# Listing a branch's loads, fixing its buffers in one tile, adding free slots, moving a product earlier and joining copies in a two-branch forward and backward kernel

## Chip, cores, metric

One core of one Trainium2 chip. The metric is the device time of one execution in microseconds (us). "1907.7 (3 runs)" is a median.

## What is computed

The reference runs a forward pass and its gradients (bf16, S = 2048, D = 1024, F = 3584), cut here to what matters:

```python
def _A_ref(q, k, v, shift_k, ssm_k, ssm_D):      # branch A: long convolution by FFT
    k_shift = ...                                # four taps over time
    kv = k_shift * v
    y_f = rfft(pad(kv)) * rfft(pad(ssm_k))       # per channel, length 2*S
    y = irfft(y_f)[:S] + kv * ssm_D
    return q * y
def _B_ref(x, W_gate, W_up, W_down):             # branch B: gated MLP
    gate, up = x @ W_gate, x @ W_up
    return (relu(gate) * up) @ W_down
xn = _layernorm(x)
out = x + _A_ref(xn, ...) + _B_ref(xn, ...)      # then the gradients of all inputs but B_x
```

## The kernel before

Both branches run on one core. The dense branch B fills TensorE with rows of eight matmuls of 512 columns: `hidden` has, for 14 blocks of weights, eight rows each of gate, up and a gradient row, and reloads the weights over a block's last rows; `grad_down` and `grad_in` follow, then the output phase (ps_o) and the input gradient (ps_x). Branch A computes its transforms as small matmuls ("passes"), for eight groups of 128 channels. It is a generator of slots, and each slot gives at most one pass for TensorE and one piece for VectorE. The dense branch counts the matmul time that it has issued, and a slot of A is taken every 1900 ns of it (`SLOT`), later every 1760 or 1250 (`DENSE`, with or without a pass). The instructions of both keep the order in which they are issued.

```python
    def run(f): ...                       # calls f, or takes the next piece of a generator
    SLOT, DENSE = 1900, (1760, 1250)
    def steps(self):
        ...
        for gi in range(self.NG):
            st = nx
            for p, d in self.slots(st, gi):          # p: pass on TensorE, d: piece on VectorE
                self.run(p)
                self.run(d)
                yield self.DENSE[p is None] if self.dense else self.SLOT
            nx = st.get("nx")
```

The loads of the next group are issued in the group's slots, wherever these fall in a block of the dense branch. Both branches issue on one queue, from SyncE:

```python
    def slots(self, st, gi):
        ...
        nx = None if last else self.load_filter(gi + 1)        # four loads of hn
        f2 = self.fwd2_pair()
        yield f2, None
        yield None, none if last else lambda: self.load_g(nx)
        yield f2, None
        yield None, none if last else lambda: self.load_xn(nx)
        # ... cut ...
        yield None, flg                                        # flip: two transposes on VectorE
        yield None, flg
        yield None, q                                          # q: a piece of a complex product
        yield ibg, q                                           # second inverse pass, reads the flips
        # ... cut ...
        yield lambda: self.tap_sums(st), q                     # sums into a PSUM tile
        if not last:
            flH = self.flip_H(nx)
            yield None, self.both(lambda: self.add_D(nx), flH)
            self.load_k(nx)
            yield None, flH
        yield None, lambda: self.tap_diagonals(st)             # reads that tile: "dg"
        Cy, Ch = self.inv_tile(), self.inv_tile()
        ia = self.inv_a_pair((Ch, Cy))                         # four passes, two PSUM tiles each
        ...
        yield ia, tg
        # ... cut: the product K*H, whose last piece stands in the slot before ...
        yield ia, tk
        # ... cut ...
        yield None, flK
        yield None, flK                                        # the next group's first pass follows
```

A's PSUM pool `ps` has two tiles. Its transform buffers B, C and GKV come from a pool of three rotating buffers, `big`; spectra and flipped data lie in a tile `arena`. The evacuation of a paired inverse pass:

```python
    self.big = self.pool("a_big", 3, side=R)
    ...
            for h in range(2):
                for k in range(2):
                    self.act(Cs[k][:, :, 2 * h:2 * h + 2, 2 * j:2 * j + 2, :],
                             ps[h][:, :, :, k].rearrange("p q m b (cp i) -> p (b cp) q m i", i=2))
```

The lines of the profile point to helpers: L72 is every matmul of A, L76 its ScalarE copies, L80 its VectorE operations, L306 its transposes, L88 its loads, L905 the rows of `hidden`.

## Time and profile before

| | before |
|---|---|
| median of 3 runs | 1907.69 us (1907.53 to 1908.38) |
| the profiled execution | 1910.69 us, span 1908.9 us |
| TensorE busy | 1884.1 us of the span |
| VectorE, ScalarE busy | 1051.5 us, 619.3 us |
| mean granted clock | 0.997 |

TensorE is the bound. So the lines to read are its waits, the time after a wait, and, where a DMA ended a wait, what stood ahead of that DMA in the queue. The prediction below shows them. "Idle before" in a group or timeline counts from the modelled end of a matmul. To size a loss I also compared starts: the time from one matmul's start to the next, less the normal step of that pair of kinds (216 ns between two 512-column matmuls, 309 from one of those to most passes, or the median of that kind of pass). I call this the start-to-start loss. The granted clock is the share of TensorE's full clock in the profile's clock record; "half clock" is a stretch recorded at 0.50.

### The profile page before, as it was taken

The page shows a single profiled execution, that of the slowest core. Times are in us where ns is not written, and L with a number is a line of the kernel's source. Part 1 is how long each engine was busy: PE and PEld are TensorE (multiplying, and loading weights), DVE is VectorE, ACT ScalarE, POOL GpSimd, SP SyncE. Part 2 cuts the span into 40 slices and gives each one's busy share as a digit, 9 for nine tenths or more (in the row PEclk, how much of TensorE's full clock was granted, in tenths as well). Part 3 has the DMA queues.
Part 4 walks back from the last instruction along what each step waited for, and adds up shares of the span by engine and source line. Part 5 has one row for each costly group of instructions (what it writes and reads, how often), then busy time and mean ns, then how long its engine had stood idle before and what let it go on. Part 6 is the DMA issues. An engine that isn't in the chain of part 4 may idle for free.

```text
span 1908.9 us, 32808 instructions
## 1 busy us (share of the span) xinstructions
PE 1884.1 (99%) x13720; PEld 855.2 (45%) x13720; DVE 1051.5 (55%) x1544; ACT 619.3 (32%) x922; POOL 14.9 (1%) x37
## 2 busy tenths in 40 slices
PE   9999999999999999999999999999999999999999
PEld 4444444344444444444444444444444544444444
DVE  6676887788788795875848757100212222222222
ACT  5655345335435535455454543211000000000000
POOL 1000000000000000000000000000000000000000
PEclk9999999999999999999999999999999999999999
DMA  9897658775675874639555434772999965555543
GB/s 250 248 238 173 169 148 179 193 193 145 168 176 153 224 221 117 168 92 255 138 147 144 137 100 145 191 253 73 259 245 237 241 148 122 122 122 122 122 121 72
DMA packets 694037, 322.93 MB, mean 169 GB/s; under 512 B 524408, under 2 KB 663424, under 8 KB 693888
## 3 DMA queue, kind: packets, MB, share of 16 engines
q1 hardware_dynamic: 683392, 299.99, 63.3%
q10 hardware_dynamic: 9216, 16.65, 2.9%
q0 software_dynamic: 1280, 4.20, 0.6%
q8 instruction: 107, 1.75, 0.4%
q14 instruction: 42, 0.34, 0.1%
HBM read 143.79 MB, written 95.44 MB: 125 GB/s over the span
## 4 chain that ended last, share of the span: by engine, by line
PE 91%; DVE 5%; issue 1%; ACT 1%; DMA 1%; SPq 0%; DVEq 0%
PE ps_x L1422 20%; PE ps_w L1195 19%; PE ps_o L1353 10%; PE ps_g L905 9%; PE ps_u L905 9%; PE ps_h L905 8%; PE ps_d L1195 8%; PE ps L72 5%; PE ps_d L1208 1%; DVE arena L306 1%; DVE ru L1009 1%; ACT C L76 1%; PE ps_w L1208 0%; ACT B L76 0%; DVE ht L1011 0%
## 5 line engine op out<-in xcount | busy, mean ns | idle before, releaser
L1195 PE MATMUL ps_w<-ugs,xn_nat 128*128 128x512 bf16 x1728 | 382.4, 379 | 0.0
L905 PEld LDWEIGHTS <-xnT 128*128 128x128 bf16 x1792 | 171.4, 98 | 217.7 <-issue 16.3
L1195 PEld LDWEIGHTS <-xn_nat 128*128 128x128 bf16 x1728 | 164.9, 98 | 201.6 <-issue 8.8
L905 PE MATMUL ps_u<-wu,xnT 128*128 128x512 bf16 x896 | 209.0, 383 | 4.2 <-DMA wu<-in_B_W_up_dram 4.1
L905 PE MATMUL ps_h<-wdT,goT 128*128 128x512 bf16 x896 | 207.6, 381 | 0.0
L905 PE MATMUL ps_g<-wg,xnT 128*128 128x512 bf16 x896 | 204.4, 380 | 1.1 <-DMA wg<-in_B_W_gate_dram 0.4
L1440 ACT ACTIVATE w<-xn,m 128x512 f32<-128x512 bf16 x32 | 24.3, 806 | 553.0 <-issue 317.2
L1422 PE MATMUL ps_x<-wuT,guT 128*128 128x512 bf16 x896 | 198.6, 379 | 0.0
L1422 PE MATMUL ps_x<-wgT,ggT 128*128 128x512 bf16 x896 | 198.6, 379 | 0.0
L1353 PE MATMUL ps_o<-wd,hT 128*128 128x512 bf16 (+1 forms) x896 | 187.6, 372 | 0.0
L1195 PE MATMUL ps_d<-g_nat,hs 128*128 128x512 bf16 x768 | 172.5, 379 | 0.0
L1345 DVE TENSOR_TENSOR ya<-ya,xe 128x1024 bf16<-128x1024 bf16 x16 | 11.1, 693 | 242.4 <-DMA xe<-xn_d 242.4
L306 DVE STREAM_TRANSPOSE arena<-C 128x1024 f32<-128x1024 f32 x48 | 89.8, 1939 | 87.6 <-ACT C L76 78.3
L1422 PEld LDWEIGHTS <-guT 128*128 128x128 bf16 x896 | 87.7, 98 | 105.7
L1422 PEld LDWEIGHTS <-ggT 128*128 128x128 bf16 x896 | 87.7, 98 | 105.5
L1353 PEld LDWEIGHTS <-hT 128*128 128x128 bf16 x896 | 87.7, 98 | 100.0
L905 PEld LDWEIGHTS <-goT 128*128 128x128 bf16 x896 | 85.1, 98 | 104.2 <-issue 6.7
L1009 DVE SCALAR_TENSOR_TENSOR ru<-ru,ps_u 128x512 bf16<-128x512 bf16 x112 | 76.4, 682 | 92.6 <-issue 43.2
L1424 DVE CUSTOM_DVE_ANT_0 gx<-ps_x,gy 128x512 f32<-128x512 f32 x32 | 22.1, 692 | 185.3 <-PE ps_x L1422 185.3
L76 ACT CAST C<-ps 128x512 bf16<-128x512 f32 (+1 forms) x160 | 96.5, 682 | 81.1 <-PE ps L72 75.3
L1299 ACT CAST wi<-ps_w 128x512 bf16<-128x512 f32 x108 | 64.1, 593 | 178.8 <-PE ps_w L1195 172.6
L1103 ACT CAST gh<-ps_h 128x512 bf16<-128x512 f32 x112 | 65.8, 588 | 154.9 <-PE ps_h L905 147.9
(154 smaller groups left out, 1663.4 us busy)
## 6 DMA issues: line engine op xcount, KB each, us to landing
ug_d<-ru SPq DMA_DIRECT2D x112, 256.0 KB, 3.6
ugs<-ug_d SPq DMA_DIRECT2D x112, 256.0 KB, 5.0
wg<-in_B_W_gate_dram SPq DMA_DIRECT2D x56, 256.0 KB, 4.2
wu<-in_B_W_up_dram SPq DMA_DIRECT2D x56, 256.0 KB, 4.3
h_d<-ht SPq DMA_DIRECT2D x112, 128.0 KB, 2.0
hs<-h_d SPq DMA_DIRECT2D x56, 256.0 KB, 5.3
out_dram<-wi SPq DMA_DIRECT2D x56, 256.0 KB, 2.9
gt<-in_grad_out_dram SPq DMA_DIRECT2D x32, 256.0 KB, 3.2
```

Source lines behind the costliest of these rows:

```text
L72: self.pri.pin(self.nc.tensor.matmul(out, lhsT=lhsT, rhs=rhs, start=start, stop=stop))
L76: self.pri.pin(self.nc.scalar.copy(out=out, in_=in_))
L306: self.pri.pin(self.nc.vector.transpose(out=df[:, c0:c0 + 32, :], in_=sf[:, c0:c0 + 32, :]))
L905: self.pri.pin(self.nc.tensor.matmul(ps[:], lhsT=xT[:, kt * P:(kt + 1) * P], rhs=w(kt), start=(kt == 0), stop=(kt == self.DT - 1)), always ...
L1009: self.pri.pin(nc.vector.scalar_tensor_tensor(out=ru[s][:, 1, :], in0=ru[s][:, 0, :], scalar=0.0, in1=ps[:], op0=ALU.is_gt, op1=ALU.mult))
L1103: self.pri.pin(nc.scalar.copy(out=gh[:], in_=ps[:]))
L1195: self.pri.pin(self.nc.tensor.matmul(ps[:], lhsT=lhsT(st), rhs=rhs(st), start=(st == 0), stop=(st == self.ST - 1)))
L1299: self.pri.pin(nc.scalar.copy(out=wo[0][:, d, :], in_=ps[:]))
L1353: nc.tensor.matmul(ps, lhsT=hT[:, kt, :], rhs=self.wd[:, kt, oc], start=(kt == 0), stop=(kt == self.FT - 1))
L1422: nc.tensor.matmul(ps, lhsT=T[:, kt, :], rhs=W[:, kt, oc], start=(i == 0), stop=(i == n - 1))
L1424: V.tensor_tensor_reduce(out=gx[:, oc], in0=ps, in1=gy[:, oc], scale=1.0, scalar=0.0, op0=ALU.add, op1=ALU.add, accum_out=m[:, ob:ob + 1])
L1440: nc.scalar.activation(out=w[:, oc], in_=xn[:, oc], func=ACT.Identity, scale=m[:, 7:8], bias=m[:, 6:7])
```

## The change

It has four parts. (1) Loads of later groups go to a list; one is issued after a slot, and none while the dense branch is in the last rows of a block (`hold`); `need` issues what must be there. (2) The buffers of A's transforms become fixed parts of one tile, instead of rotating ones. (3) Free slots are put before passes, `tap_diagonals` is moved up, and a dense slot with a pass is 1900 for 1760. (4) A paired inverse pass is copied out by two joint instructions, not four. The core of the diff:

```diff
+    def later(self, f, st):
+        self.queue.append((f, st))
+    def need(self, f, st):
+        while (f, st) in self.queue:
+            self.issue()
+    def issue(self):
+        f, st = self.queue.pop(0)
+        f(st)
@@ steps
                 self.run(p)
                 self.run(d)
+                if self.queue and not self.hold():
+                    self.issue()
@@ open_arena
-        arena = self.pool("a_are", 1, side="right").tile([P, 5, NB1 * P], BF16, name="arena")
+        arena = self.pool("a_are", 1, side="right").tile([P, 8, NB1 * P], BF16, name="arena")
+        self.Bg, self.Bk, self.H, self.GKV = rows(7), rows(6), spectrum(4), spectrum(7)
+        self.Cg, self.Ch, self.Cy = half(5), half(5), half(6)
@@ inv_a_pair
-                for k in range(2):
-                    self.act(Cs[k][:, :, 2 * h:2 * h + 2, 2 * j:2 * j + 2, :],
-                             ps[h][:, :, :, k].rearrange("p q m b (cp i) -> p (b cp) q m i", i=2))
+                self.act(self.Cs[:, :, 2 * h:2 * h + 2, 2 * j:2 * j + 2, :],
+                         ps[h][:].rearrange("p q m k b (cp i) -> p (k b cp) q m i", i=2))
@@ slots
+        yield lambda: self.tap_sums(st), q
+        self.fetch(nx, self.load_k, self.load_taps)
+        yield None, lambda: self.tap_diagonals(st)
         if not last:
-            flH = self.flip_H(nx)
+            self.need(self.load_g, nx)
+            flH = self.flip_H()
             yield None, self.both(lambda: self.add_D(nx), flH)
-            self.load_k(nx)
             yield None, flH
-        yield None, lambda: self.tap_diagonals(st)
 ...
             tk, f2H = nx["tk"], self.fwd2(H, 1)
+            yield None, tk
             yield ia, tk
 ...
         yield None, flK
         yield None, flK
+        yield None, None
@@ LnMlp
             def last_rows(sp):
+                self.hold = True
 ...
+            self.hold = False
@@
-    SLOT, DENSE = 1900, (1760, 1250)
+    SLOT, DENSE = 1900, (1900, 1250)
```

Cut: the other fetches, the order of the slots around the two final passes (one more slot between their flips and them, the next group's kvt pass two slots later), and renamed tiles.

More of the change, by code (lines that the diff above doesn't have):

```diff
@@ L62, in __init__ @@
         self.out_gk, self.out_gv, self.out_gsk, self.out_gh, self.out_gsD = out_gk, out_gv, out_gsk, out_gh, out_gsD
-        self.pools, self.pin, self.dense = [], False, False
+        self.pools, self.pin, self.dense, self.queue = [], False, False, []
     def pool(self, name, bufs, **kw):
@@ L103, in open @@
         self.ts = self.pool("a_ts", 3, side=R)
-        self.big = self.pool("a_big", 3, side=R)
         self.tmp = self.pool("a_tmp", 2, side=R)
@@ L108, in open @@
         self.ps = self.pool("a_ps", 2, space=bass.MemoryType.PSUM)
+        self.big = self.pool("a_big", 3, side=R)
         self.lnx = self.pool("a_lnx", 5, side=R)
     def open_arena(self):
-        self.pools.pop().release()
-        arena = self.pool("a_are", 1, side="right").tile([P, 5, NB1 * P], BF16, name="arena")
+        for _ in range(2):
+            self.pools.pop().release()
+        arena = self.pool("a_are", 1, side="right").tile([P, 8, NB1 * P], BF16, name="arena")
         self.flp = arena[:, 0:2, :].rearrange("p e (k c) -> p e k c", c=P)
@@ L117, in open_arena @@
         self.G, self.K = self.GK[:, :, :, 0], self.GK[:, :, :, 1]
-        self.H = arena[:, 4, :].rearrange("p (g b i c) -> p g b i c", b=2, i=2, c=P)
+        spectrum = lambda i: arena[:, i, :].rearrange("p (g b i c) -> p g b i c", b=2, i=2, c=P)
+        rows = lambda i: arena[:, i, :].rearrange("p (b cp u r i) -> p b cp u r i", cp=32, u=2, r=16, i=2)
+        half = lambda i: arena[:, i, :].rearrange("p (bc q m i) -> p bc q m i", q=4, m=8, i=2)
+        self.Bh = arena[:, 6, :].rearrange("p (b x cp n i) -> p b x cp n i", x=2, cp=16, n=NB1, i=2)
+        self.Bg, self.Bk, self.H, self.GKV = rows(7), rows(6), spectrum(4), spectrum(7)
+        self.Cg, self.Ch, self.Cy = half(5), half(5), half(6)
+        self.Cs = arena[:, 5:7, :].rearrange("p s x -> p (s x)").rearrange("p (bc q m i) -> p bc q m i", q=4, m=8, i=2)
     def close(self):
@@ L246, in ttile, with load_filter, load_rows, load_rest @@
         return self.ts.tile([P, 19, P], BF16, name=name, tag="ts")
-    def load_filter(self, gi):
-        cg = slice(gi * P, (gi + 1) * P)
-        hn = self.ld.tile([P, 2, 32, NB1], BF16, name="hn")
-        hv = self.ssm_k[cg].rearrange("(h x c) (q n) -> x h q c n", h=2, x=2, n=NB1)
+    def later(self, f, st):
[6 more added lines that the diff above has]
+        f(st)
+    def load_filter(self, st):
+        st["hn"] = self.ld.tile([P, 2, 32, NB1], BF16, name="hn")
+        self.load_rows(st, 0)
+        self.later(self.load_rest, st)
+    def load_rows(self, st, h):
+        hv = self.ssm_k[st["cg"]].rearrange("(h x c) (q n) -> x h q c n", h=2, x=2, n=NB1)
         for x in range(2):
-            for h in range(2):
-                self.load(hn[64 * x:64 * x + 64, h], hv[x, h])
-        return dict(gi=gi, cg=cg, hn=hn)
+            self.load(st["hn"][64 * x:64 * x + 64, h], hv[x, h])
+    def load_rest(self, st):
+        self.load_rows(st, 1)
     def load_g(self, st):
@@ L309, in fwd1_filter @@
     def fwd1_filter(self, st):
-        B = st["Bh"] = self.big.tile([P, 2, 2, 16, NB1, 2], BF16, name="B", tag="big")
-        hn = st["hn"]
+        B, hn = self.Bh, st["hn"]
         for k in range(2):
@@ L327, in add_D, with fwd1 @@
             rows = slice(64 * h, 64 * h + 32)
-            b0 = st["Bh"][rows].rearrange("p b x cp n i -> p b (x cp) n i")[:, 0, :, 0, :]
+            b0 = self.Bh[rows].rearrange("p b x cp n i -> p b (x cp) n i")[:, 0, :, 0, :]
             self.tt(b0, b0, st["sD"][rows, rows.start:rows.start + 64].rearrange("p (cp i) -> p cp i", i=2), ALU.add)
-    def fwd1(self, st, key, src):
-        B = st[key] = self.big.tile([P, 2, 32, 2, 16, 2], BF16, name="B", tag="big")
+    def fwd1(self, B, src):
         for r0 in range(0, 16, 8):
@@ L400, in cmul, with inv_a @@
         yield
-    def inv_tile(self):
-        return self.big.tile([P, 64, 4, 8, 2], BF16, name="C", tag="big")
-    def inv_a(self, C, Q):
+    def inv_a(self):
+        C, Q = self.Cg, self.GKV
         for j0 in range(0, 4, 2):
@@ L421, in inv_a, with inv_a_pair @@
             yield
-    def inv_a_pair(self, Cs):
+    def inv_a_pair(self):
         for j in range(4):
@@ L522, in steps @@
         yield 25000
-        nx = self.load_filter(0)
+        self.sts = [dict(gi=gi, cg=slice(gi * P, (gi + 1) * P)) for gi in range(self.NG)]
+        st = self.sts[0]
+        self.load_filter(st)
+        self.issue()
         yield 3400
-        self.load_k(nx)
-        self.load_taps(nx)
+        self.load_k(st)
+        self.load_taps(st)
         yield 3400
-        self.load_g(nx)
+        self.load_g(st)
         yield 3400
-        self.load_v(nx)
+        self.load_v(st)
         yield 6800
-        self.load_xn(nx)
+        self.load_xn(st)
         self.pin = False
@@ L535, in steps @@
         self.open_arena()
-        self.begin(nx)
-        for gi in range(self.NG):
-            st = nx
-            for p, d in self.slots(st, gi):
+        self.begin(st)
+        for st in self.sts:
+            for p, d in self.slots(st, st["gi"]):
                 self.run(p)
                 self.run(d)
+                if self.queue and not self.hold():
+                    self.issue()
                 yield self.DENSE[p is None] if self.dense else self.SLOT
-            nx = st.get("nx")
         self.small_outputs()
@@ L552, in start_kvt, with flip_H, flip_B, ahead @@
         self.tt(kvt[:, 0:16, :], st["ksh"][:], st["vt"][:], ALU.mult)
-    def flip_H(self, st):
-        return self.flip(1, st["Bh"][:].rearrange("p b x cp n i -> p (b x cp) n i"))
-    def flip_B(self, st, key, half):
-        return self.flip(half, st[key][:].rearrange("p b cp u r i -> p (b cp) (u r) i"))
+    def flip_H(self):
+        return self.flip(1, self.Bh.rearrange("p b x cp n i -> p (b x cp) n i"))
+    def flip_B(self, B, half):
+        return self.flip(half, B.rearrange("p b cp u r i -> p (b cp) (u r) i"))
     def flip_C(self, C, half):
-        return self.flip(half, C[:].rearrange("p cp q m i -> p cp (q m) i"))
+        return self.flip(half, C.rearrange("p cp q m i -> p cp (q m) i"))
+    def ahead(self, st, k):
+        gi = st["gi"] + k
+        return self.sts[gi] if gi < self.NG else None
+    def fetch(self, st, *fs):
+        if st is not None:
+            for f in fs:
+                self.later(f, st)
     def first(self, st):
-        tk, f1h = st["tk"], self.fwd1_filter(st)
+        tk, f1h, nx = st["tk"], self.fwd1_filter(st), self.ahead(st, 1)
         yield f1h, None
@@ L567, in first @@
         yield f1h, tk
+        self.fetch(nx, self.load_filter)
         yield None, self.both(lambda: self.add_D(st), tk)
         yield None, tk
-        flH = self.flip_H(st)
+        flH = self.flip_H()
         yield None, flH
@@ L576, in first @@
         yield f2H, lambda: self.gate_grad(st)
+        self.fetch(nx, self.load_xn)
         yield None, tk
         yield f2H, lambda: self.start_kvt(st)
-        f1g, f1k = self.fwd1(st, "Bg", st["gt"]), self.fwd1(st, "Bk", st["kvt"])
+        f1g, f1k = self.fwd1(self.Bg, st["gt"]), self.fwd1(self.Bk, st["kvt"])
         yield f1g, None
@@ L582, in first @@
         yield f1g, None
+        self.fetch(nx, self.load_g)
         yield None, None
         yield f1k, None
-        flG = self.flip_B(st, "Bg", 0)
+        flG = self.flip_B(self.Bg, 0)
         yield None, flG
@@ L588, in first @@
         yield None, None
-        flK = self.flip_B(st, "Bk", 1)
+        flK = self.flip_B(self.Bk, 1)
         yield None, flK
         yield None, flK
+        yield None, None
     def slots(self, st, gi):
-        last = gi + 1 == self.NG
-        G, K, H = self.G, self.K, self.H
+        G, K, H, GKV = self.G, self.K, self.H, self.GKV
         if gi == 0:
             yield from self.first(st)
-        nx = None if last else self.load_filter(gi + 1)
-        st["nx"] = nx
-        none = lambda: None
+        nx, n2 = self.ahead(st, 1), self.ahead(st, 2)
+        last = nx is None
         f2 = self.fwd2_pair()
         yield f2, None
-        yield None, none if last else lambda: self.load_g(nx)
+        yield None, None
         yield f2, None
-        yield None, none if last else lambda: self.load_xn(nx)
+        yield None, None
         yield f2, None
         yield None, lambda: self.turn(G, 0, -1, slice(0, 4))
-        GKV = self.big.tile([P, 8, 2, 2, P], BF16, name="GKV", tag="big")
-        Cg = self.inv_tile()
         q = self.cmul(H, G, True, GKV, 0)
@@ L616, in slots @@
         yield None, lambda: self.turn(G, 0, -1, slice(4, 8))
-        iaG = self.inv_a(Cg, GKV)
+        iaG = self.inv_a()
         q = self.cmul(H, G, True, GKV, 1)
@@ L620, in slots @@
         yield None, q
-        f1h = None if last else self.fwd1_filter(nx)
+        f1h = None
+        if not last:
+            self.need(self.load_filter, nx)
+            self.need(self.load_rest, nx)
+            f1h = self.fwd1_filter(nx)
         yield f1h, q
@@ L624, in slots @@
         yield f1h, q
+        self.fetch(n2, self.load_filter)
         yield None, lambda: self.turn(H, 1, 1)
@@ L629, in slots @@
         yield None, q
-        flg = self.flip_C(Cg, 0)
+        flg = self.flip_C(self.Cg, 0)
         yield None, flg
@@ L633, in slots @@
         yield None, q
-        ibg = self.inv_b(st, "gkv", 0)
-        yield ibg, q
+        yield self.inv_b(st, "gkv", 0), q
         q = self.cmul(H, K, False, K, 0)
@@ L641, in slots @@
         yield None, lambda: self.tt(gks[:, 0:16, :], gkv[:, 0:16, :], st["vt"][:], ALU.mult)
+        self.fetch(nx, self.load_v)
         gv = self.ttile("gv")
@@ L645, in slots @@
         yield lambda: self.halo(st), q
-        if not last:
-            self.load_v(nx)
         yield None, q
         yield lambda: self.tap_sums(st), q
+        self.fetch(nx, self.load_k, self.load_taps)
+        yield None, lambda: self.tap_diagonals(st)
         if not last:
-            flH = self.flip_H(nx)
+            self.need(self.load_g, nx)
+            flH = self.flip_H()
             yield None, self.both(lambda: self.add_D(nx), flH)
-            self.load_k(nx)
             yield None, flH
-        yield None, lambda: self.tap_diagonals(st)
-        Cy, Ch = self.inv_tile(), self.inv_tile()
-        ia = self.inv_a_pair((Ch, Cy))
+        ia = self.inv_a_pair()
         gk = self.ttile("gk")
@@ L661, in slots @@
         yield None, tg
-        if not last:
-            self.load_taps(nx)
         yield ia, tg
@@ L672, in slots @@
         if not last:
+            self.need(self.load_xn, nx)
             yield None, lambda: self.gate_grad(nx)
-            f1g = self.fwd1(nx, "Bg", nx["gt"])
+            self.fetch(n2, self.load_xn)
+            f1g = self.fwd1(self.Bg, nx["gt"])
         yield None, q
@@ L678, in slots @@
         yield f1g, q
+        self.fetch(n2, self.load_g)
         yield None, q
@@ L686, in slots @@
         if last:
+            yield None, None
             yield ia, None
@@ L693, in slots @@
         else:
+            self.need(self.load_k, nx)
+            self.need(self.load_taps, nx)
             self.begin(nx)
             tk, f2H = nx["tk"], self.fwd2(H, 1)
+            yield None, tk
             yield ia, tk
@@ L700, in slots @@
             yield f2H, tk
-        fly = self.flip_C(Cy, 0)
+        fly = self.flip_C(self.Cy, 0)
         yield None, fly
         yield f2H, fly
-        flh = self.flip_C(Ch, 1)
+        flh = self.flip_C(self.Ch, 1)
         yield None, flh
-        yield self.inv_b(st, "yt", 0), flh
-        yield None, tk
-        self.store_time(self.y_d, st["cg"], st["yt"])
-        yield self.inv_b_chan(st, 1), tk
+        yield None, flh
+        yield self.inv_b(st, "yt", 0), tk
         if last:
+            yield None, None
+            self.store_time(self.y_d, st["cg"], st["yt"])
+            yield self.inv_b_chan(st, 1), None
             yield None, None
@@ L713, in slots @@
             return
+        self.need(self.load_v, nx)
         yield None, lambda: self.start_kvt(nx)
-        f1k = self.fwd1(nx, "Bk", nx["kvt"])
-        flG = self.flip_B(nx, "Bg", 0)
-        yield f1k, flG
+        self.store_time(self.y_d, st["cg"], st["yt"])
+        flG = self.flip_B(self.Bg, 0)
+        yield self.inv_b_chan(st, 1), flG
+        f1k = self.fwd1(self.Bk, nx["kvt"])
         yield None, flG
@@ L720, in slots @@
         yield None, None
-        flK = self.flip_B(nx, "Bk", 1)
+        yield f1k, None
+        yield None, None
+        flK = self.flip_B(self.Bk, 1)
         yield None, flK
         yield None, flK
+        yield None, None
     def small_outputs(self):
@@ L761, in open_left @@
         self.ps = tc.alloc_tile_pool(name="b_ps", bufs=4, space=bass.MemoryType.PSUM)
-        self.ln_x, self.xn, self.todo = [], [], [[]]
+        self.ln_x, self.xn, self.todo, self.hold = [], [], [[]], False
         self.rstd = self.per.tile([P, self.ST], F32, name="rstd")
@@ L1497 @@
     a.identA = b.ident
+    a.hold = lambda: b.hold
     pri.now()
```

## The prediction

> **What bounds the kernel now.** I read the page first. Its first part:
>
> ```profile
> PE 1884.1 (99%) x13720; PEld 855.2 (45%) x13720; DVE 1051.5 (55%) x1544; ACT 619.3 (32%) x922; POOL 14.9 (1%) x37
> ```
>
> TensorE is the bound: its matmuls cover 1884.1 of 1908.9 us. The change leaves their number and sizes as they are (the order of the built instructions shows equally many on TensorE before and after), so only three things can move the end: idle time of TensorE (24.8 us, 1.3%), time at a lower clock, and switches between kinds of matmul. The view of who TensorE waited for splits the idle time:
>
> ```profile
> PE ps L72 <- DVE arena L306: 4.9, 8, 1.4
> PE ps_u L905 <- DMA wu<-in_B_W_up_dram: 4.1, 2, 2.3
> PE ps L72 <- DVE dg L80: 3.1, 3, 1.8
> PE ps L72 <- DVE arena L80: 2.9, 6, 0.8
> PE ps_warm L952 <- POOL warm L949: 1.5, 1, 1.5
> PE ps L72 <- ACT B L76: 1.1, 2, 0.6
> PE ps L72 <- DVE kvt L80: 0.8, 1, 0.8
> ```
>
> Columns: who waits, for whom, total us, times, longest. L72 is a pass of the transform branch (A), L905 a row of the dense branch (eight 512-column matmuls). Without the start (warm-up and layer norm, about 4 us, untouched), and with 0.4 us for the gate weights (wg), 17.3 us of waits lie in A's passes and at one change of weights. Busy time by stretch agrees: TensorE is idle 7.8 us of 200 to 350 us, 6.8 of 350 to 671, 3.6 of 671 to 1210, and not at all from 1210 to 1325, when A is over. The timeline of TensorE around the two largest stalls (start us, us, line, instruction, count, idle before it):
>
> ```profile
> 231.47 0.30 PE L72 MATMUL ps<-arena,IA 32*64 32x256 bf16 x4
> 233.60 0.63 PE L72 MATMUL ps<-arena,IA 32*64 32x256 bf16 x28 [1.82 <-DVE dg L80]
> 234.16 3.20 PE L905 MATMUL ps_h<-wdT,goT 128*128 128x512 bf16 x8
> ...
> 334.01 2.32 PE L905 MATMUL ps_g<-wg,xnT 128*128 128x512 bf16 x10 [0.43 <-DMA wg<-in_B_W_gate_dram]
> 338.67 1.30 PE L905 MATMUL ps_u<-wu,xnT 128*128 128x512 bf16 x4 [2.35 <-DMA wu<-in_B_W_up_dram]
> 341.69 5.28 PE L905 MATMUL ps_u<-wu,xnT 128*128 128x512 bf16 x12 [1.72 <-DMA wu<-in_B_W_up_dram]
> ```
>
> A stall is dearer than its idle time. Right after both, eight matmuls took 3.20 us and twelve 5.28, where sixteen take 3.45 to 3.63 elsewhere. The clock record has exactly two stretches at 0.50: 3.41 us from 234.6 and 6.83 us from 340.4. The cause of the second stall stands in the timeline of the DMA queue's issuer:
>
> ```profile
> 322.33 1.80 SPq L88 DMA_DIRECT2D gt<-in_grad_out_dram  x2
> 324.18 0.69 SPq L88 DMA_DIRECT2D sD<-in_A_ssm_D_dram  x1
> 324.98 1.93 SPq L898 DMA_DIRECT2D wg<-in_B_W_gate_dram  x4
> 326.96 3.32 SPq L88 DMA_DIRECT2D xt<-xn_d  x2
> 330.38 3.71 SPq L1015 DMA_DIRECT2D h_d<-ht  x2
> 334.19 0.59 SPq L1108 DMA_DIRECT2D ug_d<-ru  x1
> 334.88 0.56 SPq L1015 DMA_DIRECT2D h_d<-ht  x1
> 335.52 1.99 SPq L898 DMA_DIRECT2D wu<-in_B_W_up_dram  x4
> ```
>
> The next block's gate weights follow four loads of the next filter (hn, from 317.3) and those of gt and sD; its up weights wait behind xt and the stores, and TensorE then waits for both.
>
> [...] successive starts are 216 ns apart, and 427 in the two slow stretches. [...]
>
> **The change, part by part.** What each wait truly costs: a gap in the profile begins only at the modelled end of a matmul (379 ns after its start), while the next could start after 216, so each of the 23 gaps hides about 0.16 us: 17.3 + 23 x 0.16 = 21.0. Half clock: 3.41/2 = 1.7, and (6.83 - 1.3 idle within it)/2 = 2.8. Together **25.5 us**. Comparing start-to-start times with the normal step, gap by gap, gives 25.7; I use that split. By cause, clock included, and what the change does:
>
> - *dg* (the diagonal product that frees the PSUM tile of the tap sums): 4.0 + 1.7 clock, rounded sum 5.6. It is moved from just before the pass, behind two transposes of 1.9 us, to the slot right after the sums, two slots earlier. Removed.
> - *arena L80* (last product before the third inverse pass): 3.8. One slot is put between. Removed.
> - *wg, wu*: 5.2 + 2.7 clock = 7.9. A's loads go to a list, one a slot, and none while a block ends. In the built order of the queue no load of A stands any more between the gates of a block's last rows and its weights, except stores. Removed.
> - *arena L306* (transposes before a pass that reads them): 5.9. A free slot is put after the last transposes and one before the two final passes; the pass that reads the first inverse's transposes (1.6 of the 5.9, at 526 us) keeps its slack. 4.3 removed.
> - *kvt*: 0.9. Its pass comes two slots later. Removed.
> - *ACT B*: 1.6, two passes bunched two matmuls apart at a change of phase (903 us). In the built order no two passes are nearer than eight. Removed.
>
> A count on the built order, without any time, supports this: between a pass and the newest matmul on which its VectorE operand depends stood 9 matmuls (about one slot) before eight passes, which are just those stalled by dg (3), L80 (3), kvt (1) and the transposes at 475 us (1); after the change the smallest is 17. Joint copies: 32 passes copy with 2 instructions of 128x1024 instead of 4 of 128x512; in the timeline four took 2.05 us and two 1.93, so 32 x 0.12 = 4 us of ScalarE, which is 32% busy: nothing. Fixed parts of one tile change what waits for what, no work. Cost: 74 slots a group for 71, and a dense slot of 1900 for 1760, so A ends 216 matmuls later (count on the built order), 47 us; no TensorE work is added.
>
> Sum: 25.7 - 1.6 that stays = 24.1; I choose 2.4 for new small waits: 21.7 off 1907.7, **1886 us**.
>
> **Rivals.** *The waits move.* VectorE is 115.2 of 150 us busy in 200 to 350; removing TensorE's stalls lets the dense rows come faster and press on it, and slack 17 was not always enough (the 1.6 us at 526). The new copies into parts 5 and 6 must also wait for the filter's transpose that reads part 6, two slots before, which the rotating buffers did not need. Against it: the slots grow by 4%, so demand per us falls. It would leave 5 to 10 us, hence 1890 to 1897. *The tail.* A ends later, and the out-projection's weights (wd) load after it. Before, A ended at 1209 and the last wd landed at 1264, 55 us later; now 303 matmuls, 65 us, remain. So it fits, but thinly; a miss costs up to 10 us plus clock. *Loads come late.* A load held back over a block's end (half a block, some 22 us) could be forced out just before use; but each is listed 20 or more slots, about 38 us, ahead. *Hidden anyway:* if the removed stalls only gave time back to a later one, 1905. But TensorE's idle time does not recur elsewhere; it has nothing behind it to wait for.
>
> **Range and chances.** The floor is 1907.7 - 25.7 - about 2 (short in-pass hiccups) = 1880. Low 1881 is all removed; high 1896 is half of it kept or one new stall with its half clock. 2% faster would be 1869.5, under the floor: 1%. 2% slower needs 38 us of new waits: 2%.
>
> **What would show it.** TensorE's waits for dg, arena L80, wg/wu and kvt gone or under 1 us in all; no stretch at 0.50 after the start; idle time 24.8 down to 6 to 9; matmuls still 216 ns apart; A ending near 1235 us and TensorE unbroken at the start of ps_o. Wrong if a wait for ACT arena or DVE arena of over 5 us appears in the first half, if wd stops ps_o, or if a new stretch at 0.50 shows.

## More of the kernel before

In the trace of before the start-to-start loss is 31.4 us after the first 30 us.

## The result

| | before | after |
|---|---|---|
| median | 1908.04 us (4 runs) | 1886.26 us (1885.84 to 1886.80, 4 runs) |
| the profiled execution | 1910.69 us | 1886.80 us |
| ratio, 95% interval | | 0.9882 (0.9865 to 0.9899) |
| start-to-start loss after the first 30 us | 31.4 us | 7.2 us |
| half-clock stretches between the start and the last matmul | 2 | 0 |

A ratio is the mean time of one kernel's fast runs over that of the other's in the same rounds, so not quite the ratio of the medians. The gain is 1.2%. The first part of the page and TensorE's waits after the change:

```profile
PE 1875.4 (99%) x13720; PEld 852.3 (45%) x13720; DVE 1051.1 (56%) x1544; ACT 613.7 (33%) x858; POOL 14.9 (1%) x37
```

```profile
PE ps_warm L996 <- POOL warm L993: 1.5, 1, 1.5
PE ps L72 <- DVE arena L329: 1.1, 2, 0.6
PE ps L72 <- ACT arena L76: 0.9, 2, 0.6
PE ps_w L1254 <- DMA xn_nat<-xn_d: 0.6, 2, 0.3
```

The number of matmuls is the same. The waits for dg, wg, wu and kvt are gone, and that for a product (L80) is down to 0.3 us. Two of the lines are new: passes wait 0.9 us for ScalarE's copies (ACT arena), and ps_w waits 0.6 us for a load of xn_nat. VectorE's busy time is the same (1051.1 for 1051.5), so the gain isn't VectorE's. The pass that waited for dg at 233 us, and the rows after it, in TensorE's timeline after the change:

```profile
234.66 0.64 PE L72 MATMUL ps<-arena,IA 32*64 32x256 bf16 x32
235.23 3.63 PE L949 MATMUL ps_g<-wg,xnT 128*128 128x512 bf16 x16
238.79 0.30 PE L72 MATMUL ps<-arena,IA 32*64 32x256 bf16 x4
239.37 0.63 PE L72 MATMUL ps<-arena,IA 32*64 32x256 bf16 x28 [0.27 <-ACT arena L76]
```

The pass runs in one piece, and sixteen matmuls take 3.63 us. The next pass of the pair now waits a little for a copy. The issuer's timeline at the block end at which the weights came late before:

```profile
314.18 0.58 SPq L1153 DMA_DIRECT2D ug_d<-ru  x1
314.87 2.18 SPq L942 DMA_DIRECT2D wg<-in_B_W_gate_dram  x4
317.14 1.06 SPq L1059 DMA_DIRECT2D h_d<-ht  x2
318.63 0.54 SPq L1153 DMA_DIRECT2D ug_d<-ru  x1
320.86 0.34 SPq L1059 DMA_DIRECT2D h_d<-ht  x1
321.29 2.04 SPq L942 DMA_DIRECT2D wu<-in_B_W_up_dram  x4
```

Only the dense branch's own stores stand between the gate and the up weights; the loads of hn, gt, sD and xt, which were issued around this block end at 317 to 330 us, are elsewhere. Start-to-start losses after the first 30 us, in us, by what ended the wait:

| | before | after |
|---|---|---|
| dg | 4.0 | 0 |
| half clock | 4.2 | 0 |
| arena L80 (a product) | 3.8 | 0.5 |
| weights wg, wu | 5.2 | 0 |
| transposes (L306, after: L329) | 5.9 | 1.9 |
| kvt | 0.9 | 0 |
| ACT B | 1.6 | 0 |
| ACT arena | 0 | 1.5 |
| xn_nat | 0 | 1.0 |
| the rest, each under 0.4 | 5.8 | 2.3 |

### The profile page after: what moved, and what is told of

Its sections match the earlier page's. It is cut to its first block, busy times and chain, and to the rows that moved or that the text cites.

```text
span 1885.0 us, 32747 instructions
## 1 busy us (share of the span) xinstructions
PE 1875.4 (99%) x13720; PEld 852.3 (45%) x13720; DVE 1051.1 (56%) x1544; ACT 613.7 (33%) x858; POOL 14.9 (1%) x37
## 4 chain that ended last, share of the span: by engine, by line
PE 96%; DVE 2%; DMA 1%; issue 0%; ACT 0%; SPq 0%; DVEq 0%; ACTq 0%
PE ps_x L1468 21%; PE ps_w L1241 20%; PE ps_o L1399 10%; PE ps_g L949 10%; PE ps_h L949 10%; PE ps_u L949 10%; PE ps_d L1241 9%; PE ps L72 5%; PE ps_d L1254 1%; DVE arena L329 1%; DMA wu<-in_B_W_up_dram 0%; PE ps_r L1429 0%; DVE ru L1053 0%; DMA xn_nat<-xn_d 0%; PE ps_w L1254 0%
## 5 line engine op out<-in xcount | busy, mean ns | idle before, releaser
L76 ACT CAST arena<-ps 128x1024 bf16<-128x1024 f32 x288 | 277.7, 1018 | 200.0 <-PE ps L72 191.2
L329 DVE STREAM_TRANSPOSE arena<-arena 128x1024 f32<-128x1024 f32 x96 | 180.6, 1935 | 126.3 <-ACT arena L76 115.3
L80 DVE TENSOR_TENSOR t<-arena 128x2048 bf16<-128x2048 bf16 x96 | 114.1, 1219 | 0.4
```

Source lines behind the costliest of these rows:

```text
L76: self.pri.pin(self.nc.scalar.copy(out=out, in_=in_))
L80: self.pri.pin(self.nc.vector.tensor_tensor(out=out, in0=in0, in1=in1, op=op))
L329: self.pri.pin(self.nc.vector.transpose(out=df[:, c0:c0 + 32, :], in_=sf[:, c0:c0 + 32, :]))
```

## The experiments

Theory: each part removes the waits named for it, and the gains add, since TensorE had no other place to lose them. Rivals: the waits move on (VectorE behind them), the loads come late, or the fixed parts and the joint copies carry the gain. Eleven runs; all gave correct results. The kernels of one call ran on one chip and shared the runs of before: median 1908.79 for the first four, 1908.07 for the next four, 1906.79 for the last three.

### b_diag: before, with the diagonal product moved

```diff
         yield lambda: self.tap_sums(st), q
+        yield None, lambda: self.tap_diagonals(st)
         if not last:
 ...
-        yield None, lambda: self.tap_diagonals(st)
```

> The kernel before with the diagonal product moved to right after the tap sums, nothing else. Theory (each part removes its own waits, and they add): 5.6 us off (4.0 of waits for dg, 1.7 of half clock), so 1902.3; the stretch of half clock at 234 us is gone, the one at 340 us stays, TensorE's wait for wu stays near 4 us and that for arena L80 near 3. Rival (waits move: VectorE is the hidden bound of this stretch, so time won at dg is lost at the next transposes): 1906 to 1908, with waits for arena L306 grown by what dg lost.

Measured: 1903.05 us (1901.90 to 1904.64), ratio 0.9973 (0.9960 to 0.9985), so 5.2 us off 1908 (2.9 to 7.6). The wait for dg is gone; arena L80 still costs 3.0 us and arena L306 4.9, as before. The half-clock stretch at 234 us is gone, and one of 6.83 us begins at 334 us. The wait for wu was 2.8 us, less than the 4 expected. The waits did not move.

### b_loads: before, with the loads listed and held

The queue, `need`, `fetch` and `hold` of the change, on the rotating buffers, four copies and old slots.

> The kernel before with the loads of later groups listed, one a slot, none over a block's end; rotating buffers, slots and copies as before. Theory: 7.9 us off, so 1900; no wait for wg or wu, the half-clock stretch at 340 us gone, that at 234 us still there, dg 3, arena L80 3, arena L306 5 us of waits unchanged. Rival (the loads come late now and a pass waits for hn, gt or kp instead): a wait for a DMA in a pass of the transform branch, and under 4 us off.

Measured: 1902.30 us (1901.05 to 1902.86), ratio 0.9967 (0.9955 to 0.9980), so 6.3 us off (3.8 to 8.6). No wait for wg or wu is left and no pass waits for a DMA, so the loads don't come late. One expectation failed. TensorE's timeline around the dg wait, which this kernel keeps:

```profile
231.32 0.30 PE L72 MATMUL ps<-arena,IA 32*64 32x256 bf16 x4
233.46 0.63 PE L72 MATMUL ps<-arena,IA 32*64 32x256 bf16 x28 [1.84 <-DVE dg L80]
234.02 1.90 PE L943 MATMUL ps_h<-wdT,goT 128*128 128x512 bf16 x8
```

The wait is as long as before (1.84 for 1.82 us), but eight matmuls take 1.90 us after it, not 3.20: no half clock follows. The same wait was followed by a half clock in one execution and not in another.

### b_slots: before, with the free slots and 1900 for 1760

```diff
             tk, f2H = nx["tk"], self.fwd2(H, 1)
+            yield None, tk
             yield ia, tk
 ...
         yield None, flh
-        yield self.inv_b(st, "yt", 0), flh
-        yield None, tk
+        yield None, flh
+        yield self.inv_b(st, "yt", 0), tk
 ...
         yield None, flK
         yield None, flK
+        yield None, None
```

> The kernel before with the spare slots and 1900 for 1760 alone; loads, dg, buffers and copies as before. Theory: arena L80 3.8, arena L306 4.3, kvt 0.9 and ACT B 1.6 go, 10.6 us in all; by the count on the built order two of three dg passes keep a distance of 9 matmuls, so about 3 us of dg with its half clock stay; the loads of a group stand elsewhere against the block ends (four loads of hn now between gate and up weights), so the wait for wu stays but may change its size. 1893 to 1899. Rival (waits move to the next pass): under 5 us off, 1903 or more.

Measured: 1895.92 us (1892.74 to 1898.09), ratio 0.9934 (0.9920 to 0.9948), so 12.6 us off (9.9 to 15.3). Arena L80, kvt and ACT B are gone, and arena L306 is down from 4.9 to 1.1 us. Two waits for dg stay (2.5 us). The up weights still come late, at the same block end:

```profile
335.56 0.59 PE L913 MATMUL ps_u<-wu,xnT 128*128 128x512 bf16 x2 [2.44 <-DMA wu<-in_B_W_up_dram]
336.31 0.59 PE L913 MATMUL ps_u<-wu,xnT 128*128 128x512 bf16 x2 [0.16 <-DMA wu<-in_B_W_up_dram]
337.24 4.30 PE L913 MATMUL ps_u<-wu,xnT 128*128 128x512 bf16 x12 [0.34 <-DMA wu<-in_B_W_up_dram]
```

Free slots space the passes, but don't order the queue. Here the dg wait (1.82 us, at 236 us) was also followed by full clock, and the one for wu by a half clock of 3.41 us.

### b_three: before, with loads, diagonal product and slots

The three edits above together, still with rotating buffers and four copies.

> The kernel before with all three: loads listed and held, dg moved, spare slots; but with the rotating buffers and four copies a pass of before. Theory: the fixed parts of one tile and the joint copies give nothing, so this is as fast as the changed kernel, 1886 within 2 us. Rival (the fixed parts or the joint copies carry part of the gain): 1889 or more, with waits for C or B, or longer ScalarE waits, that the changed kernel doesn't have.

Measured: 1885.39 us (1885.29 to 1886.38), ratio 0.9881 (0.9868 to 0.9895), so 22.7 us off; the changed kernel had 0.9882. The three parts alone gave 5.2 + 6.3 + 12.6 = 24.1. The sum agrees within the intervals, and some overlap is to be expected, as the slots also removed one of three dg waits. The gain is these three parts; the fixed parts and the joint copies add nothing that shows. If anything they cost a little: the waits for ACT arena at 239 and 552 us in the changed kernel's trace (1.5 us) have no counterpart in this one, and the changed kernel timed later on the same chip (after_again) took 1886.44.

### a_nohold: the change, with loads listed but never held

```diff
-    a.hold = lambda: b.hold
+    a.hold = lambda: False
```

> The changed kernel without the hold: loads are still listed and issued one a slot, but also while a block ends. Theory: the wait for a block's weights comes from loads that stand ahead of them in the queue; in the built order four block ends now have loads of hn, xt, vt or kp between or ahead of the weights, so part of the 8 us returns: 1887 to 1894, with waits for wg or wu. Rival (listing, one a slot, was already enough): 1886 within 1, no wait for wg or wu over 0.5 us.

Measured: 1888.98 us (1888.16 to 1891.28), ratio 0.9904 (0.9889 to 0.9919), beside a_4copies at 1886.04 in the same rounds, so about 3 us of the gain hang on the hold. The issuer's timeline and then TensorE's at an early block end:

```profile
136.96 2.31 SPq L942 DMA_DIRECT2D wg<-in_B_W_gate_dram  x4
139.38 1.22 SPq L1059 DMA_DIRECT2D h_d<-ht  x2
140.70 1.57 SPq L88 DMA_DIRECT2D xt<-xn_d  x2
142.36 2.06 SPq L1153 DMA_DIRECT2D ug_d<-ru  x1
144.51 0.56 SPq L1059 DMA_DIRECT2D h_d<-ht  x1
145.16 2.02 SPq L942 DMA_DIRECT2D wu<-in_B_W_up_dram  x4
```

```profile
148.34 0.59 PE L949 MATMUL ps_u<-wu,xnT 128*128 128x512 bf16 x2 [1.71 <-DMA wu<-in_B_W_up_dram]
149.32 3.87 PE L949 MATMUL ps_u<-wu,xnT 128*128 128x512 bf16 x9 [0.38 <-DMA wu<-in_B_W_up_dram]
```

A load of xt stands between the gate and the up weights, TensorE waits 2.1 us for wu, and a half clock of 3.41 us follows. Of the four block ends with loads among the weights, only this one cost time in this trace. Listing alone is not enough.

### a_4copies: the change, with four copies a pass

```diff
-                self.act(self.Cs[:, :, 2 * h:2 * h + 2, 2 * j:2 * j + 2, :],
-                         ps[h][:].rearrange("p q m k b (cp i) -> p (k b cp) q m i", i=2))
+                for k, c in ((0, self.Ch), (1, self.Cy)):
+                    self.act(c[:, :, 2 * h:2 * h + 2, 2 * j:2 * j + 2, :],
+                             ps[h][:, :, :, k].rearrange("p q m b (cp i) -> p (b cp) q m i", i=2))
```

> The changed kernel with four copies of 128x512 in a pass instead of two of 128x1024. Theory (ScalarE has slack): 4 us more of ScalarE time and the same time in all, 1886 within 1; rival (the copies free the PSUM tiles of the next pass, so a longer copy shows on TensorE): 1888 or more, with in-pass waits for ACT arena up.

Measured: 1886.04 us (1885.70 to 1886.45), ratio 0.9887. ScalarE is busy 617.8 us for 613.7, which is the 4 us; the end is not moved.

### a_late: the change, with branch A started 40 us of matmul time later

```diff
-A_START = 45_000
+A_START = 85_000
```

> The changed kernel with the transform branch started 40 us of matmul time later, to measure the tail: it then ends 159 matmuls (34 us) before the out-projection, for 303 (65 us) now. In the changed kernel the loads of wd are through about 53 us after the branch's end. Theory (the tail is a fixed 53 us after the branch's end): TensorE stops at the first ps_o for about 19 us, plus half clock of 1.7 to 3.4, so about 1908. Rival (wd's loads would run faster or earlier, as TensorE's own traffic is less then): under 10 us more, below 1896.

Measured: 1885.40 us (1884.32 to 1885.62): no loss of time, and the rival is right (its reason was not tested). A ended 28.5 us later (1260.2 us for 1231.7) and left 38.3 us. The loads of wd were all issued 32.6 us after A's end, 36.9 in the changed kernel, and in 1285 to 1305 us the DMA engines moved 335 to 399 GB/s. The edge shows among TensorE's waits:

```profile
PE ps_o L1399 <- DMA wd<-in_B_W_down_dram: 0.9, 1, 0.9
```

So 38 us after A's end was not quite enough in this trace, where the changed kernel has 69; the 0.9 us does not show in the time, because other waits went away (those for ACT arena and one for a transpose).

### a_move: an attempt to beat the change

The largest losses left after the change are in two kinds of pass: the one that reads the first inverse's transposes (0.85 us at 211, 1.02 at 367), and the second pass of the paired inverse (0.56 at 239, 0.90 at 551). For the second, ScalarE's and VectorE's timeline of the changed kernel shows how the wait comes about (ScalarE's copy, TensorE's second piece):

```profile
550.44 1.93 ACT L76 CAST arena<-ps 128x1024 bf16<-128x1024 f32 x2 [2.40 <-DVE arena L329]
...
552.41 0.63 PE L72 MATMUL ps<-arena,IA 32*64 32x256 bf16 x28 [0.61 <-ACT arena L76]
```

The copy out of the first pass waits for VectorE's transpose, and its PSUM tile comes free late for the second pass. The edit moves both kinds one slot on and adds none:

```diff
         yield None, q
-        yield self.inv_b(st, "gkv", 0), q
+        yield None, q
         q = self.cmul(H, K, False, K, 0)
-        yield None, q
+        yield self.inv_b(st, "gkv", 0), q
         yield None, q
 ...
-        yield ia, tg
         yield None, tg
         yield ia, tg
         yield None, tg
+        yield ia, tg
+        yield None, tg
         yield None, tg
         yield None, tg
-        yield None, tg
```

> An attempt to beat the changed kernel: the pass that reads the first inverse's transposes one slot later, and the paired inverse's first two passes one slot later after the filter's transposes, with no slot added. Theory (what is left in the first half are waits of passes with too little distance: 0.85 and 1.02 us for the transposes at 211 and 367 us, 0.5 to 0.9 for the copies into part 5 and 6 at 186, 239 and 551 us): 2.5 to 3.5 us off, 1883. Rival (they move to the next pass, VectorE being over 80% busy): 1886 within 1.

Measured: 1882.29 us (1881.36 to 1883.90), ratio 0.9870 (0.9853 to 0.9886). The start-to-start loss after the first 30 us falls from 7.2 to 2.1 us. The waits of the moved passes are gone (3.3 us by the table above), and so are, which I had not foreseen, the 1.0 us for xn_nat and three of eight short in-pass losses of 0.24 to 0.29 us after 670 us. No run tells why these went. Its waits of TensorE are the start's, but for 0.3 us:

```profile
PE ps L72 <- DVE arena L80: 0.3, 1, 0.3
```

### after_again, a_move_again and a_1760, in the same rounds

> The changed kernel unaltered, to have it on the same chip and in the same rounds as the next two. 1886 within 1.

> The version with the two pairs of passes moved by a slot once more, beside the changed kernel. Theory (its gain is the 4 to 5 us by which TensorE's losses in the first and second stretch fell in its trace): 1882, 3 to 4.5 us under the changed kernel of the same rounds. Rival (the difference of the first timing lay between chips): within 1 us of it.

> The changed kernel with the old pacing of 1760 for 1900 in a slot that holds a pass. By the built order the transform branch ends 64 matmuls earlier and no two passes are nearer than eight matmuls. Theory (the pacing only sets where passes stand; the distances in slots do the work): 1886 within 1. Rival (the wider slot is what keeps passes from bunching): 1887.5 or more, with waits for ACT or VectorE in the passes after 670 us.

`a_1760` is the change with `DENSE` at (1760, 1250). Measured: the changed kernel 1886.44 us (1886.23 to 1886.64), a_move 1881.54 (1881.10 to 1882.31), a_1760 1886.62 (1886.52 to 1886.65). So a_move is 4.9 us faster than the change on one chip, with the runs well apart, a little more than expected; and the pacing alone has no effect that shows. In a_1760's trace one more transpose is waited for (1.6 us in 3 waits, for 1.1 in 2) and xn_nat no longer, so its trace is not the change's.

## Why the prediction was right

The time was 1886.26 us for 1886.0. Point by point:

- **TensorE's losses are the only thing to gain.** Right. The profiled spans differ by 23.9 us; the start-to-start losses fall by 31.4 - 7.2 = 24.2 after the start and grow by 0.4 in it. Of the 23.9, 15.2 were idle time of TensorE, which fell from 24.8 to 9.6 us (6 to 9 were expected), and 8.7 were busy time, so a stall was indeed dearer than its idle time. Two readings were rough, and nothing hangs on them: 3.5 of the 24.8 us lie after the last matmul, not in the start or in waits; and 0.16 us hidden by each gap is an average (0.07 to 0.40 in the trace).
- **dg, 5.6 us.** b_diag gave 5.2 (2.9 to 7.6). The half clock's 1.7 in it is not a fixed cost: b_loads and b_slots had the same wait without it (see the end of this section).
- **Loads, 7.9 us.** b_loads gave 6.3 (3.8 to 8.6), and a_nohold shows that the hold is part of it. The order of the queue was read rightly from the issuer's timeline. From 317.3 to 337.5 us the issuer issued one transfer after another, with at most 0.4 us between two, and its waits in that stretch are 4.1 us of these 20.2 by the profile (2.9 of them for VectorE, at one store of h_d that took 3.24 us). So what stood ahead cost mostly its issuing time. The gate weights were slow besides: 7.0 us from issue to landing, for a median of 4.2.
- **Slots: 3.8 + 4.3 + 0.9 + 1.6 = 10.6 us.** b_slots gave 12.6 (9.9 to 15.3), with one dg wait besides.
- **The count of distances on the built order** named passes that would stall: each of its eight at 9 matmuls stalled in the trace. Not among the eight were the 1.6 us at 526, the two stalls for ACT B and four of about 0.5 us for transposes after 750 us. That 17 could be short was said among the rivals, and it was: the 1.6 us expected to stay came as 0.85 and 1.02 us at other groups.
- **Copies and fixed parts: nothing.** Right, by b_three and a_4copies. The dependence of the copies on the transpose that reads part 6, named as a rival, exists: 1.5 us.
- **The tail.** That it fits was right; the margin of 10 us (65 less 55) was wrong. The step took the 55 us between A's end and the last landing for a fixed length. In a_late, where A ended 28.5 us later, the end did not move and TensorE waited 0.9 us for wd.
- **The sum** was in part lucky. Its losses of 25.7 us were read from a profiled execution of 1910.7 us, but taken off the median of 1907.7. From profile to profile the change removed 23.9 us; from median to median (1908.0 to 1886.3) 21.8. The 2.4 us allowed for new waits stood for both, what is new (1.5 for ACT arena, 1.0 for xn_nat) and that difference.

Left open at first: why the kernels whose loads may stand ahead of weights spread more (before 1904.9 to 1911.4 over all runs, b_slots 5.4 us, a_nohold 3.1) than those with held loads (b_loads 1.8, b_three 1.1, the change 1.0). The mean clock on record for each execution goes far to answer it. The 23 executions of before that were timed beside the experiments fall in order of it: 1911.2 us at 0.997 (2), 1907.7 to 1909.5 at 0.998 (12), 1905.8 to 1907.2 at 0.999 (8), 1904.9 at 1.000 (1). One stretch of 3.41 us at half clock costs 1.7 us, or 0.0009 of the mean clock, so they differ by about one stretch a step (an estimate). b_slots has 0.998 and 0.999, the change 1.000 in all its executions. So the half clock that the prediction counted (1.7 + 2.7 us) is that of its profiled execution, at 0.997; most others had less, which may be part of the 3 us between 1910.7 and the median of 1907.7 (the three executions behind that median have no clock on record). Which stalls drew a half clock in the executions without a profile stays open.

## What to carry to other kernels

When the bound engine is 99% busy, list what ended each of its waits, add what a wait costs beyond its idle time, and count on the built order how much work stands between a result and its reader: one slot was too little at eight passes here, two were short at two passes, and with a third (a_move) those two no longer waited. Where two streams of loads are issued on one queue, keep the less urgent one out of the stretch in which the urgent one reloads, rather than only spreading it: TensorE waited 2.1 us for wu in a_nohold, where loads were spread but not held, and not at all in the change. Moving a pass by a slot cost nothing here, where other work filled its place; two such moves removed their own 3.3 us of losses here, and the version with them was 4.9 us faster than the change.

## What the traces show of the clock, the steps and the queue

- Waits of 1.82 us (before), of 2.44 + 0.16 + 0.34 us (b_slots) and of 1.71 + 0.38 us (a_nohold), with some matmuls between the parts, were followed by a stretch of 3.41 us at 0.50, while waits of 1.84 and 1.82 us (b_loads, b_slots) were followed by full clock. So the length of a wait did not tell alone: 1.82 us stands on both sides. What decided between them was not shown; no run varied it by itself.
- The step between two 512-column matmuls was 216 ns at full clock and 427 ns in the stretches at 0.50 (before), with one weight load to each matmul (13720 of each). From a 512-column matmul on the whole array to a pass on a 32x64 or 64x32 part 309 ns went by, start to start, and from such a pass back 145 to 331 (before and after).
- The issuer's own waits are listed in the traces (SyncE for ps_x 213.1 us in before). At the late block end, though, they were 4.1 us of 20.2, and issuing took the rest. That block end lost 5.2 us start to start in the kernel before, and TensorE idled 2.1 us at one in a_nohold, with half clock on top (6.83 us in before, 3.41 in a_nohold).
